# Decode attention with FFN, one core: where value tiles stand in the DMA queue, and where softmax sums and head pairs stand in PSUM

## The chip, the cores and the metric

The kernel runs on one core of one Trainium2 chip. The metric is device time in microseconds (us) of one execution; less is better. Seven runs of the kernel before gave a median of 347.48 us (345.74 to 348.74). A separate execution was profiled.

Engines that matter here: TensorE (PE) for matrix products into PSUM, VectorE (DVE) for element-wise work, reductions and transposes, ScalarE (ACT) for exp and casts, and SyncE (SP), which here does nothing but issue DMAs, in program order. PEld is TensorE's loading of the stationary operand.

## The reference

Two layers, each of attention with cached keys and values and a gated FFN, are applied to 4 sequences (batch b) of one token of width 512; both layers use the same weights and the same caches.

```python
def _A_ref(x, k_cache, v_cache, wq, wo):            # 32 query heads, 8 key heads, 4096 keys, Dh = 128
    q = (x @ wq) ...                                # per head
    scores = einsum("bhqd,bhkd->bhqk", q, k) * Dh ** -0.5
    o = einsum("bhqk,bhkd->bhqd", softmax(scores), v)
    return o.reshape(B, 1, 4096) @ wo
def _B_ref(x, w_gate, w_up, w_down):
    return (gelu(x @ w_gate) * (x @ w_up)) @ w_down

for layer in (1, 2):
    x = x + _A_ref(layernorm(x), k_cache, v_cache, wq, wo)
    x = x + _B_ref(layernorm(x), w_gate, w_up, w_down)
```

## The kernel before

**Data.** A cache of one batch and one key head is two tiles of 128 x 2048 bf16, 512 KB each; so a batch has 16 key tiles and 16 value tiles. Keys go into 16 fixed buffers `KT`; they are loaded once per batch and serve layer 1 of that batch and, later, layer 2. Values are loaded for each layer anew, 128 tiles in all, through a ring of `KV_BUFS = 6` buffers (`v_t`); for the last batch's second layer the key buffers take most of them. The order in which values are used is `plan`: (batch 0, layer 1), then for b = 1, 2, 3 (b, layer 1) and (b-1, layer 2), and last (3, layer 2). `load_v` (L386) issues as many value loads as there are free buffers, always in that order. All loads go through SP's one queue, so they land in the order in which they are issued.

**Two groups.** The 8 key heads make two groups g of four. For a group, `scores` (L329) makes 16 matmuls for each half t of the keys; `soft` (L339) takes the maximum and lets ACT exponentiate; `soft_turn` (L358) transposes the probabilities `pp` and spreads the row sums as `zx`; `soft_swap` (L366) brings the probabilities into place with 16 small matmuls and an ACT cast, as `pe`. Keys must be transposed by DVE (`Keys.turn`, L319, one `kt` transpose per tile) before layer 1 can use them; layer 2 finds them transposed.

**Values.** `Values.step` (L401) uses one value tile: 16 matmuls into `ot`. With the first tile of a group it also makes the softmax denominators: a matmul of `zx` with a constant matrix (L412) into a part of the same `ot` tile, and a DVE reciprocal `rden` (L415). After each pair of heads DVE multiplies `ot` by `rden` (L425). The two pairs of a group and the sum share one PSUM tile; the pool has two such tiles.

**Order.** It is written out by hand (`manual_schedule`): each engine does its instructions in program order. After a first attention for batch 0, the main loop (L562) does for each b: layer 1's FFN of b and the queries of layer 2 (`dense`, `q_rows`), with the value steps of (b-1, layer 2) put in between as `fill`; then `attend(b, b+1)` (L431). That starts with the layer 2 scores of b for both groups (L440), and behind each half it issues four key loads of b+1 over the keys just used (L443). Then for each group: softmax of layer 2, with `build_q1` (L446) in between, which builds the group's query matrix for layer 1 of b+1 (DVE `qm`, a matmul `qe` into the pool `ps_sm`, DVE `qb`). Then come four key transposes, scores, four more, and so on, and from L480 the value steps of (b+1, layer 1) between the scores of group 1. `attend_last` (L510) is layer 2 of the last batch.

**PSUM.** Eight banks are all taken: two for scores, one for `x` of the swap, two for `ot`, two for rows, and one (`ps_sm`, one buffer) that the queries' `qe`, the layer norm's `st` and the output `y` share.

Of the kernel before, what the change touches and what calls it, by code (L numbers as in the profile page):

```python
# [8 lines left out]
FP32 = mybir.dt.float32  # L9
# [3 lines left out]
ALU = mybir.AluOpType  # L13
AX = mybir.AxisListType
RED = bass_isa.ReduceOp
P = 128
# [7 lines left out]
GH = 4  # L24
CH = 16
KV_BUFS = 6
# [3 lines left out]
def kernel(  # L30
# [13 lines left out]
    nc = tc.nc  # L44
    B, Sq, D = A_x.shape
# [3 lines left out]
    rep = Hq // Hkv  # L49
# [185 lines left out]
    def build_q1(b, g):  # L235
        q_build(q_spread(q1_bf[:, g, :, b], amask, g), g)
# [121 lines left out]
    def soft_turn(pp, ls):  # L358
        flat = pp.rearrange("p c j -> p (c j)")
        nc.vector.transpose(out=flat, in_=flat)  # L360
        zx = zp.tile([P, GH, rep], FP32, name="zx", tag="zx")
        nc.vector.tensor_scalar(out=zx[:], in0=dmask[:], scalar1=ls[:, 0:1], scalar2=None,
                                op0=ALU.mult)
        return zx

    def soft_swap(pp, pool):  # L366
        x = ps_x.tile([P, GH, NT, CH, rep], FP32, name="x", tag="x")
# [13 lines left out]
        plan += [(b, 0), (b - 1, 1)]  # L381
    plan.append((B - 1, 1))
    ring = []
    seen = {"load": 0, "use": 0}

    def load_v(upto, free=()):  # L386
        free = list(free)
        while seen["load"] < upto * VB and (free or seen["load"] < seen["use"] + KV_BUFS):
            i, n = divmod(seen["load"], VB)
            seen["load"] += 1  # L390
            kvh, t = divmod(n, NT)
            v = free.pop(0) if free else kvin.tile([P, CH, Dh], BF16, name="v_t", tag="kv")
            dq.dma_start(out=v[:], in_=cache_tile(A_v_cache, plan[i][0], kvh, t))
            ring.append(v)

    class Values:
# [4 lines left out]
        def step(self, count=1):  # L401
            for _ in range(count):
                if self.n == VB:
                    return
                assert seen["use"] == self.at * VB + self.n
                kvh, t = divmod(self.n, NT)
                self.n += 1
                g, s = divmod(kvh, GH)
                pe, zx = self.prob[g]
                if s == 0 and t == 0:  # L410
                    self.ot = ps_ot.tile([P, 2, GH, rep], FP32, name="ot", tag="ot")
                    nc.tensor.matmul(self.ot[:, 1], lhsT=mean_f[:, :], rhs=zx[:], start=True,  # L412
                                     stop=True, skip_group_check=True)
                    self.rden = grp.tile([P, GH, rep], FP32, name="rden", tag="rden")
                    nc.vector.reciprocal(out=self.rden[:], in_=self.ot[:, 1])  # L415
                load_v(self.upto)
                v = ring.pop(0)
                for i in range(CH):
                    c = t * CH + i
                    nc.tensor.matmul(self.ot[:, 0, s], lhsT=v[:, i, :], rhs=pe[:, s, c, :],  # L420
                                     start=(c == 0), stop=(c == C - 1), skip_group_check=True)
                seen["use"] += 1
                load_v(self.upto)
                if t == NT - 1 and s % 2 == 1:
                    nc.vector.tensor_tensor(  # L425
                        out=self.dst(kvh - 1).rearrange("p (k h) -> p k h", h=rep),
                        in0=self.ot[:, 0, s - 1:s + 1], in1=self.rden[:, s - 1:s + 1],
                        op=ALU.mult)


    def attend(b2, b1):  # L431
        two, first = b2 is not None, b1 == 0
        prob1, prob2 = {}, {}
        keys = Keys(b1)
        turn = keys.turn
        vals = Values(b1, 0, prob1, lambda k: OT_bf[:, k * rep:(k + 2) * rep],
                      1 if first else len(plan))
        if two:
            sc2 = [new_scores() for g in range(NG)]
            for g in range(NG):  # L440
                for t in range(NT):
                    scores(sc2[g], g, t)
                    keys.load(GH)  # L443
            for g in range(NG):
                p0 = soft(sc2[g])
                build_q1(b1, g)  # L446
                z0 = soft_turn(*p0)
                prob2[g] = (soft_swap(p0[0], p2p), z0)
            turn(4)
        else:  # L450
            load_wq(0)
            keys.load(TG)
            load_wq(1)
            keys.load(TG)
            load_v(1)
            make_identity(nc, ident_bf[:])
            build_consts()
            xT_ps = ps_sm.tile([P, KD, B], BF16, name="xT_ps", tag="sm")
            for k in range(KD):
                nc.tensor.transpose(xT_ps[:, k, :], x_bf[:B, k * P:(k + 1) * P], ident_bf[:B, :B])  # L460
            nc.vector.tensor_copy(out=XX[:, 0].rearrange("p b k -> p k b"), in_=xT_ps[:])
            ln_square(0, B)
            rstd1 = ln_rstd(B, ln_center(0, B))
            q_first(q_rows(0, B, 0), 0, rstd1)
            build_q1(0, 0)
            turn(4)
        sc1 = new_scores()
        scores(sc1, 0, 0)
        turn(4)
        scores(sc1, 0, 1)  # L470
        turn()
        p0 = soft(sc1)
        turn()
        z0 = soft_turn(*p0)
        prob1[0] = (soft_swap(p0[0], p1p), z0)
        turn(2)
        if first:
            q_first(q_rows(0, B, 1), 1, rstd1)
            build_q1(0, 1)
        vals.step(2)  # L480
        sc1 = new_scores()
        scores(sc1, 1, 0)
        turn(4)
        vals.step(3)
        scores(sc1, 1, 1)
        vals.step(1)
        p0 = soft(sc1)
        vals.step(1)
        z0 = soft_turn(*p0)
        vals.step(1)  # L490
        prob1[1] = (soft_swap(p0[0], p1p), z0)
        rows = new_rows()
        hp = 2 * rep
        if first:
            vals.step(TG)
            load_rest()
            load_v(len(plan))
            out_proj(rows, OT_bf, 0, Hq)
        else:
            for i in range(2):  # L500
                vals.step()
                out_proj(rows, OT_bf, i * hp, hp)
            vals.step(3)
            out_proj(rows, OT_bf, 2 * hp, hp)
            vals.step(3)
            out_proj(rows, OT_bf, 3 * hp, hp)
        assert vals.n == VB
        return rows, prob2

    def attend_last(b2):  # L510
        prob2 = {}
        vals = Values(b2, 1, prob2, lambda k: OT2_bf[:, k * rep:(k + 2) * rep, b2])
        free = []
        sc2 = [new_scores() for g in range(NG)]
        for t in range(NT):
            scores(sc2[0], 0, t)
            free += [KT[s][t] for s in range(GH)]
        p0 = soft(sc2[0])
        for t in range(NT):
            scores(sc2[1], 1, t)  # L520
            free += [KT[GH + s][t] for s in range(GH)]
        load_v(len(plan), free)
        z0 = soft_turn(*p0)
        prob2[0] = (soft_swap(p0[0], p2p), z0)
        p0 = soft(sc2[1])
        vals.step(3)
        z0 = soft_turn(*p0)
        prob2[1] = (soft_swap(p0[0], p2p), z0)
        vals.step(5)
        rows = new_rows()  # L530
        hp = 2 * rep
        for i in range(2):
            vals.step()
            out_proj(rows, OT2_bf, i * hp, hp)
        vals.step(3)
        out_proj(rows, OT2_bf, 2 * hp, hp)
        vals.step(3)
        out_proj(rows, OT2_bf, 3 * hp, hp)
        return rows
# [21 lines left out]
    prev = None  # L561
    for b in range(B):  # L562
        fill = (lambda n: None) if prev is None else prev.step
        dense(b, 1, rows, fill)
        ln_square(b, 1)
        fill(2)
        mv = ln_center(b, 1)
        fill(1)
        rstd = ln_rstd(1, mv)
        am = small.tile([P, QD], FP32, name="am", tag="am")  # L570
        nc.vector.tensor_scalar(out=am[:], in0=amask[:], scalar1=rstd[:, 0:1], scalar2=None,
                                op0=ALU.mult)
        qr0 = q_rows(b, 1, 0)
        fill(1)
        qm0 = q_spread(turn_rows(qr0, 512)[:, :, 0], am, 0)
        qr1 = q_rows(b, 1, 1)
        fill(1)
        q_build(qm0, 0)
        qm1 = q_spread(turn_rows(qr1, 512)[:, :, 0], am, 1)
        fill(2)  # L580
        q_build(qm1, 1)
        fill(VB)
        if b < B - 1:
            rows, prob2 = attend(b, b + 1)
            prev = Values(b, 1, prob2, lambda k, b=b: OT2_bf[:, k * rep:(k + 2) * rep, b])
        else:
            rows = attend_last(b)

    dense(0, B, rows, lambda n: None)

# [38 lines left out]
```

## Time and profile before

| | us |
|---|---|
| median of 7 runs | 347.48 (345.74 to 348.74) |
| the profiled execution | 350.32 |
| its span, from the first instruction to the last | 348.5 |
| PE busy | 218.9 (63%) |
| DVE busy | 176.2 (51%) |
| DMA from HBM | 114.56 MB, 329 GB/s over the span |
| issues of value tiles / key tiles | 128 / 64, 512 KB each |
| idle PE ahead of value matmuls, ended by a DVE reciprocal (L415) | 9.6, 15 times |
| idle PE ahead of value matmuls, ended by a DVE multiply of a pair (L425) | 3.0, 6 times |
| idle PE ahead of value matmuls, ended by a value tile's DMA | 13.3, 18 times |
| idle PE ahead of scores, ended by a key transpose on DVE (L324) | 20.8, 28 times |

How to read the profile: "busy" is the time in which an engine had an instruction, not the time that bounds the kernel. In rows of instructions the columns are start, duration, engine, line, operation, output tile <- input tiles, shapes and count; in square brackets stands how long the engine was idle before, and which instruction or DMA ended that idle time. In rows by stretches of the span, the count of instructions stands in brackets behind each busy time. The page cuts the span into 40 slices of 8.7 us; a digit is the busy share in tenths.

In the main loop three stretches are alike, one for each of b = 0, 1, 2: the scores of layer 2 begin at 96.5, 166.8 and 238.9 us, the first key load behind them is issued at 98.4, 168.0 and 240.2 us, and the first value load after the keys at 123.6, 196.9 and 267.6 us.

### The profile page before, as it was taken

The numbers are of one execution on the slowest core, as the hardware profiler recorded it, in microseconds if no ns is written. First come the engines' busy times: TensorE is split into PE (matmuls) and PEld (weight loads), VectorE is DVE, ScalarE is ACT, GpSimd is POOL, SyncE is SP. The second block draws the span as 40 slices with busy tenths as digits, with TensorE's granted clock in tenths as the row PEclk, the third lists the DMA queues.
The fourth block names the chain that finished last, engine by engine and source line by source line (L and its number), as shares of the span: only waits on it lengthen the run. The fifth ranks groups of instructions, "written<-read, shape, count | busy, mean of one in ns | idle before, by whom it ended". The sixth has DMA issues, their size and how long they took to land.

```text
span 348.5 us, 8051 instructions
## 1 busy us (share of the span) xinstructions
PE 218.9 (63%) x3522; PEld 113.8 (33%) x3522; DVE 176.2 (51%) x476; ACT 24.2 (7%) x54; POOL 0.7 (0%) x6
## 2 busy tenths in 40 slices
PE   0452563242665487699735577999364689987673
PEld 0110342010221144445311344654112445545431
DVE  5658620032559872245587930644899405435043
ACT  0003010000011101000110110000201100003000
POOL 0000000000000000000000000000000000000000
PEclk9999999999996555555855555557855555558555
DMA  7999999999459969999999599999997999999700
GB/s 268 393 406 401 407 380 321 353 402 374 185 154 413 393 226 324 355 371 346 342 414 405 206 301 350 412 379 341 408 409 265 320 355 401 318 405 410 291 2 0
DMA packets 35779, 115.09 MB, mean 330 GB/s; under 512 B 3224, under 2 KB 9120, under 8 KB 35744
## 3 DMA queue, kind: packets, MB, share of 16 engines
q1 hardware_dynamic: 35744, 114.58, 88.5%
q8 instruction: 27, 0.44, 0.5%
q14 instruction: 8, 0.07, 0.0%
HBM read 114.56 MB, written 0.00 MB: 329 GB/s over the span
## 4 chain that ended last, share of the span: by engine, by line
DMA 34%; PE 33%; DVE 22%; SPq 5%; issue 3%; ACT 1%; ACTq 0%
DMA kt<-in_A_k_cache_dram 14%; DMA v_t<-in_A_v_cache_dram 14%; DVE kt L324 10%; PE ot L420 10%; PE sc L335 8%; DMA wd_sb<-in_B_w_down_dram 5%; SPq L122 3%; PE rows L205 3%; PE rows L255 3%; PE rows L269 3%; PE rows L299 3%; DVE rt L195 2%; DVE m L341 2%; DVE pp L360 2%; PE ot L412 1%
## 5 line engine op out<-in xcount | busy, mean ns | idle before, releaser
L420 PE MATMUL ot<-pe,v_t 128*128 128x4 bf16 x1888 | 63.1, 167 | 26.9 <-DMA v_t<-in_A_v_cache_dram 13.3
L324 DVE STREAM_TRANSPOSE kt<-kt 128x1024 f32<-128x1024 f32 x64 | 75.7, 1219 | 6.8 <-DMA kt<-in_A_k_cache_dram 6.3
L420 PEld LDWEIGHTS <-v_t 128*128 128x128 bf16 x1888 | 58.5, 104 | 56.9 <-issue 31.9
L335 PE MATMUL sc<-kt,qb 128*32 128x512 bf16 x512 | 63.9, 567 | 20.8 <-DVE kt L324 20.8
L195 DVE STREAM_TRANSPOSE rt<-rows 128x512 f32<-128x512 f32 (+1 forms) x30 | 20.8, 692 | 42.9 <-PE rows L255 18.3
L335 PEld LDWEIGHTS <-qb 128*32 128x32 bf16 x512 | 18.3, 121 | 54.5 <-issue 34.5
L425 DVE TENSOR_TENSOR OT_bf<-ot,rden 128x8 bf16<-128x8 f32 x32 | 5.2, 163 | 50.3 <-PE ot L420 50.3
L371 PE MATMUL x<-pp,ident_bf 128*32 128x128 bf16 x256 | 8.4, 266 | 31.8 <-DVE pp L360 31.8
L255 PE MATMUL rows<-wo_sb,OT_bf 128*1 128x512 bf16 (+1 forms) x160 | 20.5, 609 | 10.9 <-DMA wo_sb<-in_A_wo_dram 9.9
L341 DVE TENSOR_REDUCE m<-sc 128x1 f32<-128x512 f32 x16 | 11.0, 688 | 24.7 <-PE sc L335 24.7
L354 ACT ACTIVATE pp<-sc,nm 128x512 bf16<-128x512 f32 x16 | 11.0, 687 | 163.2 <-DVE junk L350 144.2
L205 PE MATMUL rows<-wq_sb,xn_bf 128*1 128x512 bf16 (+1 forms) x160 | 18.6, 620 | 4.9 <-DMA wq_sb<-in_A_wq_dram 4.4
L371 PEld LDWEIGHTS <-ident_bf 128*32 128x32 bf16 x256 | 6.1, 112 | 36.2 <-issue 31.8
L360 DVE STREAM_TRANSPOSE pp<-pp 128x512 bf16<-128x512 bf16 x16 | 11.2, 702 | 6.4 <-ACT pp L354 6.4
L299 PE MATMUL rows<-wd_sb,H_bf 128*1 128x512 bf16 (+1 forms) x70 | 9.3, 619 | 4.7 <-DMA wd_sb<-in_B_w_down_dram 3.6
L229 DVE TENSOR_TENSOR qb<-qe,amask 128x256 bf16<-128x256 f32 x16 | 6.8, 424 | 9.9 <-PE qe L226 9.9
L374 ACT CAST pe<-x 128x512 bf16<-128x512 f32 x16 | 9.4, 586 | 23.6 <-PE x L371 23.6
L269 PE MATMUL rows<-wu_sb,xn_bf 128*1 128x448 bf16 (+1 forms) x80 | 8.4, 569 | 2.9 <-DMA wu_sb<-in_B_w_up_dram 2.9
L412 PE MATMUL ot<-zx,mean_f 128*128 128x16 f32 x32 | 9.5, 377 | 0.0
L269 PE MATMUL rows<-wg_sb,xn_bf 128*1 128x448 bf16 (+1 forms) x80 | 8.3, 567 | 1.8 <-DVE r L176 1.2
L412 PEld LDWEIGHTS ot<-zx,mean_f 128*128 128x128 f32 x32 | 7.8, 305 | 4.1 <-issue 3.9
L226 PE MATMUL qe<-qm,t_bf 128*128 128x64 bf16 x16 | 3.4, 214 | 9.0 <-DVE qm L216 9.0
(63 smaller groups left out, 102.6 us busy)
## 6 DMA issues: line engine op xcount, KB each, us to landing
v_t<-in_A_v_cache_dram SPq DMA_DIRECT2D x118, 512.0 KB, 7.3
kt<-in_A_k_cache_dram SPq DMA_DIRECT2D x64, 512.0 KB, 10.6
kt<-in_A_v_cache_dram SPq DMA_DIRECT2D x10, 512.0 KB, 10.1
wq_sb<-in_A_wq_dram SPq DMA_DIRECT2D x2, 2048.0 KB, 8.0
wo_sb<-in_A_wo_dram SPq DMA_DIRECT2D x4, 1024.0 KB, 13.8
wg_sb<-in_B_w_gate_dram SPq DMA_DIRECT2D x1, 1792.0 KB, 13.5
wu_sb<-in_B_w_up_dram SPq DMA_DIRECT2D x1, 1792.0 KB
wd_sb<-in_B_w_down_dram SPq DMA_DIRECT2D x1, 1792.0 KB, 18.8
```

Source lines behind the costliest of these rows:

```text
L195: nc.vector.transpose(out=t.rearrange("p n j -> p (n j)"), in_=rows[:, :n])
L205: nc.tensor.matmul(rows[j * QS:j * QS + nb, :], lhsT=xn_bf[:, k, bs], rhs=w, start=(k == 0), stop=(k == KD - 1))
L255: nc.tensor.matmul(rows[r0:r0 + nb, :], lhsT=lhsT, rhs=wo_sb[:, i, :], start=(i < QD), stop=(i >= Hq - QD))
L269: nc.tensor.matmul(rows[j * QS:j * QS + nb, :KF * QS], lhsT=xn_bf[:, k, bs], rhs=w[:, j], start=(k == 0), stop=(k == KD - 1))
L299: nc.tensor.matmul(rows[r0:r0 + nb, :], lhsT=H_bf[:, c, :], rhs=wd_sb[:, c, :], start=(c < QD), stop=(c >= KF - QD))
L324: nc.vector.transpose(out=words, in_=words)
L335: nc.tensor.matmul(sc[s * QS:(s + 1) * QS], lhsT=QB[g][:, w0:w0 + 2 * W], rhs=kt[:, :, be // 2, :, be % 2], start=(t == 0 and be == 0), st ...
L341: nc.vector.tensor_reduce(out=m[:], in_=sc.rearrange("p c j -> p (c j)"), axis=AX.X, op=ALU.max)
L360: nc.vector.transpose(out=flat, in_=flat)
L371: nc.tensor.matmul(x[a * QS:(a + 1) * QS, s], lhsT=ident_bf[:, s * QS:(s + 1) * QS], rhs=pT[:, a], start=True, stop=True, skip_group_check ...
L412: nc.tensor.matmul(self.ot[:, 1], lhsT=mean_f[:, :], rhs=zx[:], start=True, stop=True, skip_group_check=True)
L420: nc.tensor.matmul(self.ot[:, 0, s], lhsT=v[:, i, :], rhs=pe[:, s, c, :], start=(c == 0), stop=(c == C - 1), skip_group_check=True)
```

## The change

- While b is 1 or 2 (`0 < b < B - 1`), value loads are held back: of (b+1, layer 1) only three tiles (`KV_BUFS // 2`) may be issued ahead of the keys of b+1. `attend` lifts the limit behind its sixteen key loads and issues the rest there.
- The softmax sum has functions of its own, `soft_den` and `soft_recip`; the sum goes into the shared pool `ps_sm` and is made where the softmax is, no longer with the first value tile.
- `ot` holds one pair of heads; each pair takes the next of the two buffers.
- The query matrix of group 1 for layer 2 (`q_build(qm1, 1)`) is no longer built ahead of the last value steps; it comes between the scores of group 0 and those of group 1.
- In `attend`, the query matrix for layer 1 of b+1 is built behind the softmax of its group, no longer in the middle of it.

```diff
     def soft_turn(pp, ls):
...
+    def soft_den(zx):
+        den = ps_sm.tile([P, GH, rep], FP32, name="den", tag="sm")
+        nc.tensor.matmul(den[:], lhsT=mean_f[:, :], rhs=zx[:], start=True, stop=True)
+        return den
+
+    def soft_recip(den):
+        rden = zp.tile([P, GH, rep], FP32, name="rden", tag="rden")
+        nc.vector.reciprocal(out=rden[:], in_=den[:])
+        return rden
...
-        while seen["load"] < upto * VB and (free or seen["load"] < seen["use"] + KV_BUFS):
+        while seen["load"] < min(upto * VB, seen["cap"]) and (free or seen["load"] < seen["use"] + KV_BUFS):
...
-                pe, zx = self.prob[g]
-                if s == 0 and t == 0:
-                    self.ot = ps_ot.tile([P, 2, GH, rep], FP32, name="ot", tag="ot")
-                    nc.tensor.matmul(self.ot[:, 1], lhsT=mean_f[:, :], rhs=zx[:], start=True,
-                                     stop=True, skip_group_check=True)
-                    self.rden = grp.tile([P, GH, rep], FP32, name="rden", tag="rden")
-                    nc.vector.reciprocal(out=self.rden[:], in_=self.ot[:, 1])
+                pe, rden = self.prob[g]
+                if s % 2 == 0 and t == 0:
+                    self.ot = ps_ot.tile([P, 2, rep], FP32, name="ot", tag="ot")
...
@@ attend, layer 2 of b @@
                 for t in range(NT):
                     scores(sc2[g], g, t)
                     keys.load(GH)
+                if g == 0:
+                    last_q()
+            seen["cap"] = len(plan) * VB
+            load_v(len(plan))
             for g in range(NG):
                 p0 = soft(sc2[g])
-                build_q1(b1, g)
                 z0 = soft_turn(*p0)
-                prob2[g] = (soft_swap(p0[0], p2p), z0)
+                pe = soft_swap(p0[0], p2p)
+                den = soft_den(z0)
+                qm = q_spread(q1_bf[:, g, :, b1], amask, g)
+                prob2[g] = (pe, soft_recip(den))
+                q_build(qm, g)
             turn(4)
@@ attend, layer 1 of b+1 @@
-        prob1[0] = (soft_swap(p0[0], p1p), z0)
-        turn(2)
+        pe = soft_swap(p0[0], p1p)
+        den = soft_den(z0)
+        turn()
+        prob1[0] = (pe, soft_recip(den))
+        turn()
...
-        prob1[1] = (soft_swap(p0[0], p1p), z0)
+        prob1[1] = (soft_swap(p0[0], p1p), soft_recip(soft_den(z0)))
@@ main loop @@
+        if 0 < b < B - 1:
+            seen["cap"] = plan.index((b + 1, 0)) * VB + KV_BUFS // 2
...
         qm1 = q_spread(turn_rows(qr1, 512)[:, :, 0], am, 1)
-        fill(2)
-        q_build(qm1, 1)
         fill(VB)
         if b < B - 1:
-            rows, prob2 = attend(b, b + 1)
+            rows, prob2 = attend(b, b + 1, lambda: q_build(qm1, 1))
...
         else:
-            rows = attend_last(b)
+            rows = attend_last(b, lambda: q_build(qm1, 1))
```

In `attend_last`, `last_q()` stands behind the scores of group 0, ahead of their softmax, and both groups get their denominators with the softmax, as `soft_recip(soft_den(z0))`.

More of the change, by code (lines that the diff above doesn't have):

```diff
@@ L360, in soft_turn @@
         nc.vector.transpose(out=flat, in_=flat)
-        zx = zp.tile([P, GH, rep], FP32, name="zx", tag="zx")
+        zx = grp.tile([P, GH, rep], FP32, name="zx", tag="zx")
         nc.vector.tensor_scalar(out=zx[:], in0=dmask[:], scalar1=ls[:, 0:1], scalar2=None,
@@ L383 @@
     ring = []
-    seen = {"load": 0, "use": 0}
+    seen = {"load": 0, "use": 0, "cap": len(plan) * VB}
     def load_v(upto, free=()):
         free = list(free)
-        while seen["load"] < upto * VB and (free or seen["load"] < seen["use"] + KV_BUFS):
+        while seen["load"] < min(upto * VB, seen["cap"]) and (free or seen["load"] < seen["use"] + KV_BUFS):
             i, n = divmod(seen["load"], VB)
@@ L419, in step @@
                     c = t * CH + i
-                    nc.tensor.matmul(self.ot[:, 0, s], lhsT=v[:, i, :], rhs=pe[:, s, c, :],
+                    nc.tensor.matmul(self.ot[:, s % 2], lhsT=v[:, i, :], rhs=pe[:, s, c, :],
                                      start=(c == 0), stop=(c == C - 1), skip_group_check=True)
@@ L426, in step, with attend @@
                         out=self.dst(kvh - 1).rearrange("p (k h) -> p k h", h=rep),
-                        in0=self.ot[:, 0, s - 1:s + 1], in1=self.rden[:, s - 1:s + 1],
-                        op=ALU.mult)
-    def attend(b2, b1):
+                        in0=self.ot[:], in1=rden[:, s - 1:s + 1], op=ALU.mult)
+    def attend(b2, b1, last_q=None):
         two, first = b2 is not None, b1 == 0
@@ L508, in attend, with attend_last @@
         return rows, prob2
-    def attend_last(b2):
+    def attend_last(b2, last_q):
         prob2 = {}
@@ L517, in attend_last @@
             free += [KT[s][t] for s in range(GH)]
+        last_q()
         p0 = soft(sc2[0])
@@ L523, in attend_last @@
         z0 = soft_turn(*p0)
-        prob2[0] = (soft_swap(p0[0], p2p), z0)
+        prob2[0] = (soft_swap(p0[0], p2p), soft_recip(soft_den(z0)))
         p0 = soft(sc2[1])
@@ L527, in attend_last @@
         z0 = soft_turn(*p0)
-        prob2[1] = (soft_swap(p0[0], p2p), z0)
+        prob2[1] = (soft_swap(p0[0], p2p), soft_recip(soft_den(z0)))
         vals.step(5)
```

## The prediction, before the changed kernel ran

> **What bounds the kernel now.** I read the page's slices first, then the rows of the three alike stretches on DVE and PE, then PE's waits, since no engine is full over the span.
>
> ```profile
> DMA  7999999999459969999999599999997999999700
> GB/s 268 393 406 401 407 380 321 353 402 374 185 154 413 393 226 324 355 371 346 342 414 405 206 301 350 412 379 341 408 409 265 320 355 401 318 405 410 291 2 0
> ```
>
> A full queue moves some 410 GB/s, so 114.56 MB need about 279 us; the span is 348.5. The slices with 185 and 154, 206 and 265 GB/s are where the queue has gaps. The first lies around the layer 2 scores of b = 0 (about 91 to 98 us: keys wait for scores); the others lie behind the last keys of b = 0, 1, 2 (121-126, 193-198, 265-269 us): all six value buffers are full and no value step has freed one. The three tiles that are moved behind the keys aim at the last two of these. One tile takes 1.28 us of a full queue (0.524 MB at 410 GB/s), so three are 3.8 us.
>
> Whether that is won depends on what the keys wait for. The b = 1 stretch, DVE alone:
>
> ```profile
> 169.65 0.69 DVE L341 TENSOR_REDUCE m<-sc 128x1 f32<-128x512 f32 x1 [2.54 <-PE sc L335]
> ...
> 172.77 0.70 DVE L360 STREAM_TRANSPOSE pp<-pp 128x512 bf16<-128x512 bf16 x1
> 173.40 0.20 DVE L362 TENSOR_SCALAR zx<-dmask,ls 128x16 f32<-128x16 f32 x1
> 173.50 0.68 DVE L341 TENSOR_REDUCE m<-sc 128x1 f32<-128x512 f32 x1
> ...
> 175.78 0.71 DVE L360 STREAM_TRANSPOSE pp<-pp 128x512 bf16<-128x512 bf16 x1
> 176.41 0.19 DVE L362 TENSOR_SCALAR zx<-dmask,ls 128x16 f32<-128x16 f32 x1
> 177.42 8.93 DVE L324 STREAM_TRANSPOSE kt<-kt 128x1024 f32<-128x1024 f32 x7 [0.81 <-DMA kt<-in_A_k_cache_dram]
> 187.31 2.53 DVE L324 STREAM_TRANSPOSE kt<-kt 128x1024 f32<-128x1024 f32 x2 [0.96 <-DMA kt<-in_A_k_cache_dram]
> ```
>
> DVE is done with both softmaxes at 176.6 and the first key holds it only 0.81 us, then the keys pace it (1.28 us each, the DMA's pace, against 1.14 where they lie ready). So DVE was less than a microsecond from being the bound itself. In b = 0 it is: nine transposes run without a gap from 106.17 us (10.25 us), the keys being there.
>
> The value part of the same stretch:
>
> ```profile
> 196.23 1.02 PE L420 MATMUL ot<-pe,v_t 128*128 128x4 bf16 x32 [1.38 <-DVE rden L415]
> 200.59 0.12 DVE L425 TENSOR_TENSOR OT_bf<-ot,rden 128x8 bf16<-128x8 f32 x1
> 200.76 0.57 PE L420 MATMUL ot<-pe,v_t 128*128 128x4 bf16 x16 [0.74 <-DVE OT_bf L425]
> 206.28 0.62 PE L371 MATMUL x<-pp,ident_bf 128*32 128x128 bf16 x16 [1.75 <-DVE pp L360]
> 206.83 0.61 PE L412 MATMUL ot<-zx,mean_f 128*128 128x16 f32 x2
> 207.89 0.56 PE L420 MATMUL ot<-pe,v_t 128*128 128x4 bf16 x16 [0.44 <-DVE rden L415]
> 216.06 0.58 PE L420 MATMUL ot<-pe,v_t 128*128 128x4 bf16 x16 [0.75 <-DMA v_t<-in_A_v_cache_dram]
> ```
>
> PE waits for DVE at the sum (1.38, 0.44) and at the pair (0.74), and from about 212 us for value DMAs. Up to the next scores it is close to DMA-bound: counting the queue's packets in order of issue, the last layer 2 tile is in about 164.5 us plus a completion of 1.5 us or so, and is used at 166.35.
>
> **The change, part by part.**
>
> *Softmax in `attend` (removed from its middle: `build_q1`; added: `den`, reciprocal).* Before, from `pp` to the next group's `m` 0.73 us pass (172.77 to 173.50). Now DVE goes `pp`, `zx`, `qm`, reciprocal, `qb`, then `m`, and each waits for PE. Nearest rows: `pp` to swap 0.76; swap to end of the sum's matmul 0.74 where PE is quick (317.04 swap, 317.38 + 0.40 L412), 1.16 where it is slow (206.28 to 207.44); to DVE 0.04, reciprocal 0.26, back to PE 0.05, `qe` to `qb` 0.27, `qb` to the next operation 0.34. Sum 2.46, so **1.73 us more per group, 3.5 for two**; with the slow figure 4.3. Here a rule of the Trainium skill speaks against the change: "PSUM — Partial Sum Buffer", section "PSUM bank collisions raise a hardware error", wants TensorE and VectorE kept apart by bank, not by address. `den` and `qe` take the one buffer of `ps_sm` in turn, so `qe` cannot overlap the reciprocal's read. Were only the data dependences to count, `qe` would run under the reciprocal and the sum would be about 2.1 (2.8 for two groups); by the rule 3.5. No row of before shows this pair; I take 3.5. In exchange nothing is gained in the middle: ACT's exp (0.69) was what covered `build_q1`, and ends when `pp` starts anyway (102.38 and 102.41 in b = 0). Only in b = 1 and 2, where `qe` sat behind the scores of group 1, is `pp` 0.8 and 0.5 sooner. Behind DVE in this order stand the key transposes, and for them wait the scores.
>
> *Query build of group 1 moved.* PE no longer waits for `qm1` ahead of the last value step (0.65 us). The scores of group 0 start some 1.1 us sooner in b = 0, 0.6 to 0.7 in b = 1 and 2 (a value tile's landing allows no more). But `qb1` now stands on DVE ahead of `m` and waits for those scores: 0.05 + 0.27 + 0.34 = 0.66 us later. Net on `m`: -0.5 in b = 0, about 0 in b = 1 and 2, +0.66 in `attend_last`.
>
> *Three value tiles behind the keys.* With three fewer ahead, the first key of b = 1 can be there 3.8 us sooner, at about 173.6; a lone load takes 3.3 us (value issued at 123.59, in by 126.9), so an issue at 167.3 holds that. SP issues sixteen keys, then these three; later value loads queue behind them, but their buffers come free only about 195 us. The queue has no gap there. What it releases is worked out with DVE: b = 1: `m` 169.7, `pp` 172.0, second `m` 174.4, `pp` 176.7, first transpose **179.2** instead of 177.4. Eight at 1.14 us end at 188.3; before 188.57: **-0.3**. b = 2 likewise: `m` 242.0, first transpose 251.5 (before 249.09), eight end at 260.6 (before 259.3): **+1.3**. b = 0, where the limit does not hold: -0.5 + 3.5 = **+3.0**. So the keys' head start is mostly spent on waiting for DVE.
>
> *Sum and pairs apart.* The two waits on the key part go: the value steps no longer wait, but the next scores still need the last key transpose (200.65 us), so only the step between is won (200.76 to 201.33): 0.57. The reciprocal ahead of group 1's values: 0.44, of which ACT's cast of `pe` still holds about 0.1: 0.33. Together **-0.9 in each of b = 0, 1, 2** and -0.4 in the first attention. Against a naive credit: the Trainium skill, same page, "Summary: rules for kernel authors", says to read PSUM from another bank than the running matmuls use; by it all waits on `rden` and on the pairs, 9.6 + 3.0 = 12.6 us, could go. The rows say otherwise: most are followed by a wait for a transpose or a value DMA. In layer 2's steps the matmul L412 and its wait go as well (157.33 to 158.22, 0.9 us), but the tiles used there are bound by DMA (two or three tiles later PE is within 0.3 us of their landing; at 309.71 it waits 0.48): I cost this at nothing beyond the 0.6 to 0.7 taken above.
>
> *`attend_last`.* `m` +0.66; `m` of group 1 now stands behind the reciprocal (+1.65 in all), its swap at 321.7 instead of 320.06; then five value steps, but no L412 with its wait (1.03) and no pair wait (0.27): **+0.6**.
>
> **Sum.** b = 0 with the first attention: +3.0 - 0.9 - 0.4 = +1.7; b = 1: -0.3 - 0.9 = -1.2; b = 2: +1.3 - 0.9 = +0.4; end +0.6. In all **+1.5 us**: span 350.0 for 348.5. The profiled execution took 350.32, 2.84 above the median of the seven, and I carry the difference over: 347.48 + 1.5 = **349.0 us**.
>
> **Rivals.**
> - *The keys bind, DVE keeps up* (faster). If the handoffs cost 0.5 us per group rather than 1.73, transposes start at 176.7 in b = 1 and at 249.0 in b = 2, each stretch is 2.5 us shorter than in my sum, `attend_last` breaks even: 1.5 - 7.5 - 0.6 = -6.6, **341 us**. For it: the gaps in the DMA row. Against: DVE was free only at 176.6 even before. It decides from about 1.2 us per group on, where the change breaks even.
> - *Values gain* (slightly faster). Buffers come free 1.2 us sooner at 196.23 and more loads are in flight; if the 0.9 us of each of the three L412 in layer 2 and the whole 1.2 reach the end once per b, 1.5 - 3 = -1.5: **346 us**. Against: the waits for value DMAs around 212 to 216 us.
> - *PE stays slow* (slower). The scores of b = 0 run at half speed from 96.5 to 99.8 and then twice as fast; a break of 0.7 us between the groups could put this off. Then the swap comes 0.4 later and the sum takes 1.16: +0.8 in each stretch, **351.5 us**.
> - That the change doesn't do what it says can be ruled out for the order: three loads do stand behind the keys in the changed program.
>
> **How the numbers follow.** Mine 0.5 (own range 347.3 to 350.5), keys bind 0.13, values gain 0.17, PE slow 0.2. The measurement tells about 0.3% from none, 1.04 us. Slower: 0.34 of mine and the slow rival; faster: the first rival and most of the second; the rest is the same: 0.54, 0.26, 0.2. The range, 345 to 351.8, leaves out the first rival and little else: 2.8 to 4.3 us for the handoffs in three stretches gives -2 to +2.5 around 349, the values the rest below.
>
> **What would show it.** Right: first key transpose of b = 1 near 179 and of b = 2 near 251 us less the shift so far, ended by `qb` and not by a key DMA; transposes at 1.14 us; full DMA in the slices behind the keys; no wait for `rden` on PE. Wrong: a key transpose that still waits for DMA at 174 to 177 us, or `m` of group 1 less than 2 us behind `pp`.

## The result, and the profile after

The changed kernel is slower: median 350.65 us (22 runs) against 347.5 us (57 runs) before. The ratio of comparable runs is **1.0074** (95% interval 1.0053 to 1.0096), so 2.6 us (1.8 to 3.3). Ratios leave out slow runs, those more than 1.5% above the fastest of their kernel, and so differ from the ratio of the medians, which are of all runs. The prediction was 1.5 us slower, 349.0 us. The profiled execution took 350.93 us with a span of 349.2 us; before it was 350.32 and 348.5. The 57 executions of the kernel before lie between 343.5 and 351.1 us, so the two profiles, 0.6 us apart, tell where time went, not how much in all.

The page of the changed kernel, busy share and rate of the DMA queue in 40 slices of 8.7 us:

```profile
DMA  7999999999499589999799899997997899999900
GB/s 272 389 409 394 409 368 353 356 400 377 160 327 412 221 284 304 352 393 362 251 399 412 291 309 312 412 403 256 390 402 306 277 332 409 343 363 375 381 20 0
```

The slice behind the last keys of b = 1 (the 23rd) moved 291 GB/s instead of 206, the one of b = 2 (the 31st) 306 instead of 265: the three tiles do fill much of the gaps that they aim at. But the queue lost at least as much ahead of the keys: the 20th slice moved 251 GB/s instead of 342, the 28th 256 instead of 341. A key load can be issued only when the scores have used its buffer, and in b = 1 the first was issued at 167.7 us, before at 168.0; with three values fewer ahead of it, the queue ran short there. The gap was moved, not closed. The keys did come sooner, and yet the span is no shorter. The reason for that stands on VectorE; b = 1, rows in order of time (start, duration, engine, line, operation, output <- inputs, and in brackets the idle time before and what ended it):

```profile
172.22 0.71 DVE L360 STREAM_TRANSPOSE pp<-pp 128x512 bf16<-128x512 bf16 x1 [0.93 <-ACT pp L354]
172.86 0.19 DVE L362 TENSOR_SCALAR zx<-dmask,ls 128x16 f32<-128x16 f32 x1
172.96 0.27 DVE L216 TENSOR_TENSOR qm<-q_bf,amask 128x64 bf16<-128x64 bf16 x1
173.76 0.26 DVE L373 RECIPROCAL rden<-den 128x16 f32<-128x16 f32 x1 [0.53 <-PE den L368]
174.30 0.42 DVE L229 TENSOR_TENSOR qb<-qe,amask 128x256 bf16<-128x256 f32 x1 [0.28 <-PE qe L226]
174.64 0.68 DVE L341 TENSOR_REDUCE m<-sc 128x1 f32<-128x512 f32 x1
...
179.03 0.42 DVE L229 TENSOR_TENSOR qb<-qe,amask 128x256 bf16<-128x256 f32 x1 [0.30 <-PE qe L226]
179.37 10.25 DVE L324 STREAM_TRANSPOSE kt<-kt 128x1024 f32<-128x1024 f32 x9
190.45 0.69 DVE L341 TENSOR_REDUCE m<-sc 128x1 f32<-128x512 f32 x1 [0.83 <-PE sc L335]
```

From `pp` to the next group's `m` 2.42 us pass where it was 0.73; two idle times in between are new, each a wait for a small TensorE result. The first key transpose starts at 179.37 instead of 177.42, directly behind `qb`; no row of this stretch waits for a key DMA any more, and nine transposes run at 1.14 us. The keys came early and lay there.

The value part of the same stretch, TensorE and VectorE:

```profile
198.04 1.44 PE L426 MATMUL ot<-pe,v_t 128*128 128x4 bf16 x48
...
200.61 0.13 DVE L431 TENSOR_TENSOR OT_bf<-ot,rden 128x8 bf16<-128x8 f32 x1
200.74 1.86 PE L335 MATMUL sc<-kt,qb 128*32 128x512 bf16 x13 [0.54 <-DVE OT_bf L431]
...
207.02 0.57 PE L426 MATMUL ot<-pe,v_t 128*128 128x4 bf16 x16
...
215.24 0.59 PE L426 MATMUL ot<-pe,v_t 128*128 128x4 bf16 x16 [1.05 <-DMA v_t<-in_A_v_cache_dram]
```

The first three value steps of group 0 now run together, ahead of the pair's multiply at 200.61, and the first value matmul of group 1 starts without waiting for the reciprocal. What TensorE waits for in all, as engine, line, what it waited for, then total us, times and the longest:

```profile
PE ot L426 <- DMA v_t<-in_A_v_cache_dram: 22.7, 35, 1.7
PE sc L335 <- DVE kt L324: 18.9, 28, 1.7
...
PE sc L335 <- DVE qb L229: 2.6, 5, 0.5
...
PE qe L226 <- DVE rden L373: 2.1, 6, 0.3
```

No value matmul waits for a reciprocal now (9.6 us before), but the waits for value DMAs have grown from 13.3 to 22.7 us. In the eleven profiles with the new PSUM part they lie between 17.7 and 24.4 us, in the three with the old one between 13.3 and 17.2: much of the 12.6 us that were taken off at the sums and the pairs came back as another wait.

By stage, worked out from the starts and ends of rows of three profiles (us; `order_back` is the changed kernel with one part undone, see below; three numbers are b = 0, 1, 2):

| stage | before | after | order_back |
|---|---|---|---|
| start to the layer 2 scores of b = 0 | 96.5 | 93.6 | 92.9 |
| those scores' start to the first key transpose | 9.7 / 10.6 / 10.2 | 12.5 / 13.6 / 14.0 | 9.0 / 11.2 / 10.5 |
| first to end of last key transpose | 21.2 / 23.2 / 22.3 | 21.3 / 21.3 / 21.3 | 21.6 / 21.6 / 21.6 |
| to the next layer 2 scores | 39.4 / 38.2 / 38.8 | 38.4 / 37.3 / 39.4 | 38.5 / 37.5 / 39.9 |
| last layer 2 scores to the end | 38.3 | 36.4 | 36.6 |

The second line is the loss: 9.6 us in three stretches. The third line is what the early keys give: 2.8 us. The differences of these two profiles add up to 0.6 us; the measured 2.6 us come from the many runs.

### The profile page after: what moved, and what is told of

Same layout as the page of the kernel before. It is cut to its first block, busy times and chain, and to the rows that moved or that the text cites. A ratio compares the mean times of both kernels' runs of the same rounds, so it can differ in the third digit from the quotient of the medians.

```text
span 349.2 us, 8052 instructions
## 1 busy us (share of the span) xinstructions
PE 220.3 (63%) x3522; PEld 112.9 (32%) x3522; DVE 174.7 (50%) x476; ACT 24.2 (7%) x54; POOL 0.7 (0%) x6
## 4 chain that ended last, share of the span: by engine, by line
DMA 41%; DVE 27%; PE 21%; SPq 5%; ACT 3%; issue 3%; ACTq 0%
DMA v_t<-in_A_v_cache_dram 25%; DVE kt L324 14%; DMA kt<-in_A_k_cache_dram 8%; PE sc L335 7%; DMA wd_sb<-in_B_w_down_dram 5%; PE ot L426 4%; DMA kt<-in_A_v_cache_dram 3%; SPq L122 3%; DVE pp L360 3%; DVE m L341 3%; ACT pp L354 2%; PE x L381 2%; PE rows L255 1%; PE rows L299 1%; DVE qb L229 1%
## 5 line engine op out<-in xcount | busy, mean ns | idle before, releaser
L335 PE MATMUL sc<-kt,qb 128*32 128x512 bf16 x512 | 67.7, 562 | 23.1 <-DVE kt L324 18.9
L426 PE MATMUL ot<-pe,v_t 128*128 128x4 bf16 x1888 | 63.5, 167 | 24.3 <-DMA v_t<-in_A_v_cache_dram 22.7
L324 DVE STREAM_TRANSPOSE kt<-kt 128x1024 f32<-128x1024 f32 x64 | 73.9, 1210 | 4.1 <-DMA kt<-in_A_k_cache_dram 4.1
L195 DVE STREAM_TRANSPOSE rt<-rows 128x512 f32<-128x512 f32 (+1 forms) x30 | 20.8, 692 | 38.5 <-PE rows L255 17.5
L299 PE MATMUL rows<-wd_sb,H_bf 128*1 128x512 bf16 (+1 forms) x70 | 6.8, 474 | 4.7 <-DMA wd_sb<-in_B_w_down_dram 3.6
L373 DVE RECIPROCAL rden<-den 128x16 f32<-128x16 f32 x16 | 4.1, 257 | 9.8 <-PE den L368 9.8
L368 PE MATMUL den<-zx,mean_f 128*128 128x16 f32 x32 | 8.5, 344 | 0.0
L154 PE MATMUL st<-XX,mean_f 128*128 128x8 f32 (+1 forms) x20 | 5.8, 366 | 3.5 <-DVE XX L149 3.5
## 6 DMA issues: line engine op xcount, KB each, us to landing
kt<-in_A_v_cache_dram SPq DMA_DIRECT2D x10, 512.0 KB, 11.2
wo_sb<-in_A_wo_dram SPq DMA_DIRECT2D x4, 1024.0 KB, 12.6
```

The lines of the kernel that those rows point to most:

```text
L195: nc.vector.transpose(out=t.rearrange("p n j -> p (n j)"), in_=rows[:, :n])
L324: nc.vector.transpose(out=words, in_=words)
L335: nc.tensor.matmul(sc[s * QS:(s + 1) * QS], lhsT=QB[g][:, w0:w0 + 2 * W], rhs=kt[:, :, be // 2, :, be % 2], start=(t == 0 and be == 0), st ...
L426: nc.tensor.matmul(self.ot[:, s % 2], lhsT=v[:, i, :], rhs=pe[:, s, c, :], start=(c == 0), stop=(c == C - 1), skip_group_check=True)
```

## The experiments

All ratios are to the kernel before, with 95% intervals; times are medians of all runs.

**The held-back values alone** (`cap_only`), on the kernel before:

```diff
-        while seen["load"] < upto * VB and (free
+        while seen["load"] < min(upto * VB, seen["cap"]) and (free
...
                     keys.load(GH)
+            seen["cap"] = len(plan) * VB
+            load_v(len(plan))
             for g in range(NG):
...
+        if 0 < b < B - 1:
+            seen["cap"] = plan.index((b + 1, 0)) * VB + KV_BUFS // 2
```

> The kernel before with the held-back value tiles alone (three ahead of the keys, three behind, for b = 1 and 2). Theory 1, VectorE's handoffs: DVE is free for the keys at 176.6 us in b = 1 and at 248.6 in b = 2, the keys lie ready, eight transposes at 1.14 us end 2.8 and 1.6 us sooner: 3 to 4.5 us faster than before, first key transpose of b = 1 straight behind the softmax. Theory 2, the held-back values cost the time: values arrive late, slower than before by 1 us or more.

Measured: 346.09 us, ratio 0.998 (0.9947 to 1.0013). Neither theory's number came. In its profile b = 1 does what theory 1 says: from the layer 2 scores' start to the end of the eighth transpose it takes 19.2 us instead of 21.7. In b = 2, where DVE had only 0.4 us to spare before, it takes 20.0 instead of 20.4, and the value steps that follow take 1.3 us longer (40.1 against 38.8). So the keys' head start is real, but only 0.7 us of it survives by the ratio, and the interval holds zero.

**The query build back in the middle of the softmax** (`order_back`), on the changed kernel:

```diff
                 p0 = soft(sc2[g])
+                build_q1(b1, g)
                 z0 = soft_turn(*p0)
-                pe = soft_swap(p0[0], p2p)
-                den = soft_den(z0)
-                qm = q_spread(q1_bf[:, g, :, b1], amask, g)
-                prob2[g] = (pe, soft_recip(den))
-                q_build(qm, g)
-            turn(4)
+                prob2[g] = (soft_swap(p0[0], p2p), z0)
+            turn(2)
+            for g in range(NG):
+                den = soft_den(prob2[g][1])
+                turn(1)
+                prob2[g] = (prob2[g][0], soft_recip(den))
```

> The changed kernel with the layer 1 query build back in the middle of attend's softmax, and both softmax sums behind the second key transpose. Theory 1: from pp to the next m 0.7 us instead of 2.4, first key transpose about 3.4 us sooner in each of b = 0, 1, 2; 6 to 9 us faster than the changed kernel, so 341 to 345 us and faster than before. Theory 2: values or keys bind, so less than 1.5 us come of it, 349 to 350.5 us.

Measured: 342.18 us, ratio 0.9825 (0.9747 to 0.9903): 8.7 us better than the changed kernel (0.0249 of 347.5), and faster than before. The interval is wide. Once more on another chip:

> order_back once more on the same chip as the two above, to compare with: 341 to 343 us.

Measured: 343.3 us, ratio 0.9872 (0.982 to 0.9924), 0.3 us above what was expected. By this measurement the gain over the changed kernel is 7.0 us; so it is 7 to 9 us. The rows of `order_back` on VectorE in b = 1, from the first profile:

```profile
169.36 0.70 DVE L360 STREAM_TRANSPOSE pp<-pp 128x512 bf16<-128x512 bf16 x1
169.98 0.20 DVE L362 TENSOR_SCALAR zx<-dmask,ls 128x16 f32<-128x16 f32 x1
170.08 0.69 DVE L341 TENSOR_REDUCE m<-sc 128x1 f32<-128x512 f32 x1
...
173.10 3.49 DVE L324 STREAM_TRANSPOSE kt<-kt 128x1024 f32<-128x1024 f32 x3
176.52 0.22 DVE L373 RECIPROCAL rden<-den 128x16 f32<-128x16 f32 x1
```

`pp` to `m` is 0.72 us again. The reciprocals stand behind transposes, 0.22 us each and with nothing to wait for, since the sum was made under a transpose of 1.2 us. Theory 2, less than 1.5 us, is refuted: it was neither values nor keys that kept the changed kernel slow.

**All six value tiles ahead of the keys again** (`no_cap`), on the changed kernel: the two lines of the main loop that set the limit are left out.

> The changed kernel with all six value tiles ahead of the keys again. Theory 1: with transposes that start at 179 us the keys' head start is hardly used, so 0 to 1.5 us slower than the changed kernel. Theory 2: 1.5 us or more faster than the changed kernel.

Measured: 350.05 us, ratio 1.0106 (1.0052 to 1.016), against 1.0074: within theory 1's 0 to 1.5 us: the difference is 1.1, and the intervals overlap, so no effect is shown.

**The query build of layer 2 back ahead of the last value steps** (`q1_early`), on the changed kernel:

```diff
+        fill(2)
+        q_build(qm1, 1)
         fill(VB)
...
-            rows, prob2 = attend(b, b + 1, lambda: q_build(qm1, 1))
+            rows, prob2 = attend(b, b + 1, lambda: None)
```

> The changed kernel with the layer 2 query build of group 1 back ahead of the last value steps. Theory 1: scores start 0.65 us later, but the maximum no longer waits 0.66 us behind qb; b = 0 loses 0.5, the last attention gains 0.66: within 0.7 us of the changed kernel. Theory 3, this move is what made it slower: 1.5 us or more faster than the changed kernel.

Measured: 352.81 us, ratio 1.0197 (1.0144 to 1.0251), which no theory had expected, from six runs and with a profile that ends where the changed kernel's does (349.3 us). So it was measured again:

> q1_early once more, since its first measurement lay 1.2% above the changed kernel while its profile shows the same span. Theory 1: the query build's place is worth nothing that can be measured, 349.5 to 351.5 us. Theory 6: 352.5 us and up again.

Measured: 350.06 us over 22 runs, ratio 1.0081 (1.0046 to 1.0115). The first number did not repeat; whether it was scatter or the chip isn't shown. Its interval was too narrow for what it was used for, a warning for the other six-run ratios. The same move on the good order (`order_q1`):

> order_back with the layer 2 query build of group 1 back ahead of the last value steps. Theory 1: the 0.65 us that scores start later and the 0.66 us that m no longer waits cancel, within 1 us of order_back. Theory 6, the move is itself a gain (q1_early was slower than the changed kernel, which theory 1 did not expect): 2 us or more slower than order_back.

Measured: 341.88 us, ratio 0.9799 (0.9734 to 0.9864). This is level with `order_back`, so theory 6 falls; the place of this build makes no difference that can be measured.

**How the loss splits.** `half_den` is the changed kernel with `build_q1(b1, g)` back behind `soft` and no query build later; the sum and its reciprocal stay in the softmax:

```diff
                 p0 = soft(sc2[g])
+                build_q1(b1, g)
                 z0 = soft_turn(*p0)
                 pe = soft_swap(p0[0], p2p)
-                den = soft_den(z0)
-                qm = q_spread(q1_bf[:, g, :, b1], amask, g)
-                prob2[g] = (pe, soft_recip(den))
-                q_build(qm, g)
+                prob2[g] = (pe, soft_recip(soft_den(z0)))
```

> The changed kernel with the layer 1 query build back in the middle of attend's softmax, but with the sum's matmul and the reciprocal still in the softmax ahead of the next group's m. Theory 1 (each handoff between VectorE and TensorE costs its own time): from pp to the next m 1.7 us (0.76 + 0.74 + 0.04 + 0.26 less 0.1), half way between 0.7 and 2.4; some 4 us faster than the changed kernel and 3 to 5 us slower than order_back: 344 to 347 us. Theory 4 (only the query matmul's wait for the shared bank is dear): within 1.5 us of order_back, 341 to 343.5 us.

Measured: 347.51 us over 22 runs, ratio 1.0003 (0.9975 to 1.0032), 0.5 us above the range expected. Its rows in b = 1, group 0:

```profile
169.10 0.70 DVE L360 STREAM_TRANSPOSE pp<-pp 128x512 bf16<-128x512 bf16 x1
169.72 0.19 DVE L362 TENSOR_SCALAR zx<-dmask,ls 128x16 f32<-128x16 f32 x1
170.62 0.26 DVE L373 RECIPROCAL rden<-den 128x16 f32<-128x16 f32 x1 [0.71 <-PE den L368]
170.80 0.63 DVE L341 TENSOR_REDUCE m<-sc 128x1 f32<-128x512 f32 x1
```

1.70 us from `pp` to `m`, as worked out. In group 1, where the first key transpose comes next instead of `m`, it is 2.14 us. `build_late` makes the opposite move on the kernel before: only the query build goes behind the swap.

```diff
                 p0 = soft(sc2[g])
-                build_q1(b1, g)
                 z0 = soft_turn(*p0)
                 prob2[g] = (soft_swap(p0[0], p2p), z0)
+                build_q1(b1, g)
```

> The kernel before with one move alone: the layer 1 query build behind the softmax's swap in attend. Theory 1: from pp to the next m 1.8 us (0.76 + 0.41 + 0.27 + 0.34) instead of 0.7; the transposes then run at 1.14 us and make some of it good in b = 1 and 2: 1.5 to 4 us slower than before, 349 to 351.5 us. Theory 4: no change, since no bank is waited for.

Measured: 350.52 us, ratio 1.0104 (1.0067 to 1.014), 3.6 us slower. Its rows:

```profile
173.07 0.71 DVE L360 STREAM_TRANSPOSE pp<-pp 128x512 bf16<-128x512 bf16 x1 [0.93 <-ACT pp L354]
...
174.42 0.42 DVE L229 TENSOR_TENSOR qb<-qe,amask 128x256 bf16<-128x256 f32 x1 [0.36 <-PE qe L226]
174.76 0.68 DVE L341 TENSOR_REDUCE m<-sc 128x1 f32<-128x512 f32 x1
```

1.69 us. The interval occurs six times in a run: in group 0 from `pp` to the next `m`, in group 1 from `pp` to the first key transpose, for three b. Where nothing is waited for it is 0.73 us in both. The excess over that, added up over the six, makes a scale. Two kernels are set against `order_back`, by its first and its second measurement, and `build_late` against the kernel before:

| kernel | group 0, `pp` to `m`, us | group 1, `pp` to first `kt`, us (b = 0 / 1 / 2) | excess of the six, us | ratio | slower by, us |
|---|---|---|---|---|---|
| order_back | 0.73 | 0.74 / 0.73 / 0.74 | 0 | 0.9825, again 0.9872 | |
| half_den | 1.70 | 2.14 / 2.14 / 2.14 | 7.1 | 1.0003 | 6.2 or 4.6 |
| after | 2.42 | 2.87 / 2.45 / 2.87 | 11.1 | 1.0074 | 8.7 or 7.0 |
| before | 0.73 | 0.74 / 1.64 / 1.24, the last two with a wait for a key's DMA | | 1 | |
| build_late | 1.69 | 1.92 / 1.94 / 1.93 | 6.5 | 1.0104 | 3.6 |

Each handoff costs its own time, and between a half and nine tenths of it reaches the end. Theory 4, that only the wait for the shared bank is dear, falls with `half_den`, 4.6 to 6.2 us behind `order_back`. How much of the 0.72 us between `half_den` and the changed kernel is the bank's alone was not tried apart: all eight banks are taken.

**The parts without the handoffs.** `psum_only` is `order_back` without the limit and with the early query build, so the kernel before with the PSUM part alone:

> The kernel before with the PSUM part alone (sums and pairs apart, the sums behind the second key transpose): six values ahead of the keys, both query builds where they were before. Theory 1: 0.9 us in each of b = 0, 1, 2 and 0.4 in the first attention, 3 us faster than before, 343.5 to 345.5 us; what is gained in layer 2's value steps is hidden by value DMAs. Rival: those waits count too, 5 us or more faster.

Measured: 343.05 us, ratio 0.9864 (0.9817 to 0.991): 4.7 us (3.1 to 6.4) faster than before, between the two expectations. `order_nocap` is `order_back` without the limit alone:

> order_back without the held-back values: all six value tiles ahead of the keys. Theory 1: DVE is free for the keys at 173.1 us in b = 1, where the first key would be about 172.5 us instead of 168.6, so most of the keys' head start was surplus: 0 to 2 us slower than order_back, 342 to 344 us. Theory 5, holding values back is what makes order_back fast: 3 us or more slower, 345 us and up.

Measured: 342.61 us, ratio 0.986 (0.9811 to 0.9909): 1.2 us behind `order_back`'s first measurement and level with its second. Most of the keys' head start is surplus here too, as theory 1 says, and what the held-back values give beside the PSUM part lies within the scatter.

**The last attention mended** (`order_last`), on `order_back`:

```diff
-        prob2[0] = (soft_swap(p0[0], p2p), soft_recip(soft_den(z0)))
+        pe = soft_swap(p0[0], p2p)
+        den = soft_den(z0)
         p0 = soft(sc2[1])
+        prob2[0] = (pe, soft_recip(den))
         vals.step(3)
...
+        if b == B - 1:
+            fill(2)
+            q_build(qm1, 1)
         fill(VB)
...
-            rows = attend_last(b, lambda: q_build(qm1, 1))
+            rows = attend_last(b, lambda: None)
```

> order_back with the last attention mended: the query build of group 1 ahead of the last value steps for the last batch alone, and group 0's reciprocal behind group 1's maximum. Theory 1: m of group 0 0.66 us and m of group 1 some 1.6 us sooner behind the scores' start, 0.5 to 1.6 us faster than order_back, so the fastest of all, 340 to 341.5 us. If value DMAs bind at the end: no difference.

Measured: 341.42 us, ratio 0.9829 (0.9775 to 0.9883), among the others of its kind. In its profile the end, from the last layer 2 scores on, takes 37.1 us, in the two of `order_back` 36.6 and 38.6. A gain isn't shown.

The version that beats both kernels is thus the changed one with the softmax's order put back: `order_back`, `order_q1`, `order_last` and `order_nocap` all lie at 341.4 to 343.3 us, and these runs do not rank them. Nor do they tell them from `psum_only` (343.05), the kernel before with the PSUM part alone.

## Why the prediction was right

The direction and the range held, by the mechanism named: the change wins on keys that come sooner and on PSUM waits, and loses more on VectorE's handoffs.

- **Handoffs, +1.73 per group, 3.5 per b.** Measured +1.69 in group 0 of each b (2.42 for 0.73), and +2.13, +1.71 and +2.13 in group 1: 3.8, 3.4 and 3.8 per b. The quick figure for the sum's matmul was right for four of the six (0.40 us at 173.32 and 178.02); in group 1 of b = 0 the slow one came (0.61 us at 104.49, at a granted clock of 0.50), and with it 0.4 us more, as again in b = 2 (0.61 at 250.50). `qe` did wait for the reciprocal, 2.1 us in six waits. That follows from the program's one buffer; no run lets the two overlap, so the rule on banks itself isn't tested here.
- **Key head start.** The first transpose of b = 1 came at 179.37 us (forecast 179.2), of b = 2 at 252.05 (251.5), and eight transposes of b = 1 ended at 188.49 (forecast 188.3, before 188.55), of b = 2 at 261.17 (260.6). The agreement is in part luck, since the scores had started 1.1 and 0.9 us sooner than before, not 0.6 to 0.7. Counted from the scores' start, the first transposes came 13.6 and 14.0 us behind, with 13.0 and 13.3 forecast. The rival that DVE keeps up is refuted. Its break-even should have read 1.5 us per group, not 1.2: 1.23 us less per group was to be worth 8.1 us, so 0.23 us less makes up for 1.5. `cap_only` shows that even with DVE as it was before, only 0.7 us would have come of 7.7 us of moved transfers.
- **PSUM part.** This term was probably too small: 0.9 in each b and 0.4 at the start make 3.1 us; `psum_only` measured 4.7, with 3.1 at the edge of its interval. In the profiles the stage to the next scores gains 0.6 to 1.3 us per b, near the 0.9 taken. The rest is at both ends of the span. At the start, the layer 2 scores of b = 0 begin at 92.7 to 95.4 us (mean 93.7) in the eleven profiles with the new PSUM part and at 95.9 to 96.5 (mean 96.2) in the three with the old one: 2.5 us, of which I had 0.4, and 1.1 for the later query build where that is in. The last value loads ahead of the weights are issued only 0.2 to 1.1 us sooner; but the first weight behind them lands 1.9 us sooner in the mean (61.2 for 63.1 us), and why is open. The naive credit of 12.6 us is refuted: the waits went, and 4.7 us reached the end.
- **`attend_last`, +0.6.** Wrong in sign. `m` of group 1 was indeed late (8.2 us behind the scores' start, before 6.8), but from those scores to the end it takes 36.4 us instead of 38.3. One part is a wait of TensorE for nothing that the profile shows: 2.0, 1.6 and 2.0 us in the three profiles with the old PSUM part, 0.8 or less in ten of the eleven with the new one. The PSUM part does not remove it, though: in `order_last`, where the reciprocal no longer holds `m` up, it is back with 1.6 us. So TensorE seems to wait there for something that comes at its own time, which would hide a later `m`, and would leave `order_last` nothing to gain; what it is isn't shown. The forecast had carried the wait over as fixed.
- **Value steps.** The stage behind b = 2 did not gain its 0.9 us but lost 0.6 (39.4 for 38.8): value DMAs bind there (from 271 to 313 us TensorE waits 6.0 us for them, before 2.4), as the second rival's counter-evidence had it.
- **PE slow.** Right in part. The scores of b = 0 took 2.08 and 1.98 us per group, where the first group had taken 3.45. With no break either, that first group took 2.04 us in `cap_only` and 3.60 in `order_q1`, so the break isn't shown to decide it either way. In b = 1 and 2, group 0's scores took 3.6 us in the changed kernel's profile, at a granted clock of 0.50, where they had taken 2.7 and 3.0 at 0.70 and 0.62. And two of the six sums were slow, as said above. What this cost in all was not measured.

By the stages of the table, the forecast's terms, taken together, were -1.5 us to the first layer 2 scores, +9.6 to the first transposes, -3.2 for the transposes, -4.0 to the next scores and +0.6 at the end; the profiles show -2.9, +9.6, -2.8, -1.4 and -1.9. At the two ends 3.9 us of gain were missing from the forecast, in the value stages it had 2.6 us too many, and that these offset each other is luck. So is the exact 9.6: it was forecast as 4.1, 2.5 and 3.1 for the three b and came as 2.8, 3.0 and 3.8. The forecast of 1.5 us against 2.6 measured is thus right in its direction and its main mechanism, not by its terms.

## What to carry to other kernels

A transfer that is brought forward is worth only as much as the engine that consumes it is free sooner than the data used to come: look up when that engine is free, before counting the gap in the queue. And look where the gap goes: here it moved from behind the keys to ahead of them. On an engine that works in program order, an operation that waits for another engine's small result costs a large part of its round trip if the critical work stands behind it (here a half to nine tenths); put it behind work that does not need it, as the reciprocal behind a key transpose. Work that fills the wait for an exponential is not free to move: `build_late` moved one query build and lost 3.6 us.

## What the runs showed of the hardware

- Moving value loads alone did not shorten the value stage: in `cap_only` it took 39.3, 38.7 and 40.1 us, before 39.4, 38.2 and 38.8.
- Counted by the packets of the queue in the profile of before, value tiles of 512 KB came 1.4 to 1.9 us apart between 153 and 166 us, where only a few were outstanding, against 1.25 to 1.3 us while eight key loads stood in the queue. The load issued at 123.59 us, into an empty queue, had its last packet in 3.3 us later.
- A round trip between VectorE and TensorE of tiny operations is long beside its work: `zx` ends at 173.05 us and `m` starts at 174.64, 1.6 us for a sum, a reciprocal and a query matrix that keep VectorE busy for 0.95 us.
- The same 32 score matmuls took 2.0 us at a granted clock of 1.00 (b = 0) and 3.6 us at 0.50 (b = 1), both in the changed kernel. The row doesn't tell all: before, those of b = 0 took 3.45 us, and the clock reads 1.00 there too.
- A six-run median lay 2.75 us from the same kernel's median over 22 runs on another chip (352.81 and 350.06).
